# Where the first expert's transposed rows are kept, and in which order the last two attention blocks are routed, in a fused attention, expert and feed-forward kernel

## The chip, the cores and the metric

One NeuronCore of a Trainium2 chip runs the whole kernel. The metric is the device time of one execution in microseconds (us). Five engines work side by side, each through its own queue in order: TensorE (PE, with PEld for its weight loads), VectorE (DVE), ScalarE (ACT), GpSimd (POOL) and SyncE (SP, which only issues transfers here). A matmul shows in the trace as PE; transfers are issued by SP and, where the rows are picked by an index, by POOL.

## The reference, cut to what matters

Attention with four sink keys and a window of 128, then a top-1 mixture of eight experts with a capacity, then a feed-forward layer with a squared relu:

```python
keep = is_sink | in_window                        # q, k, v: 2 x 8 heads x 768 x 64
a = softmax(where(keep, q @ k.T / 8, -1e9)); attn = a @ v
x = attn.transpose(0, 2, 1, 3).reshape(1536, 512)
logits = x @ w_gate; e = argmax(logits, 1); gate = softmax(logits)[e]
disp[e, rank of the token within e] = x[token]    # up to 384 rows of each expert
y = relu(disp @ w1[e]) @ w2[e]                    # 512 -> 1024 -> 512
out_moe[token] = gate * y[e, rank]
h = relu(out_moe @ w_in); out = (h * h) @ w_out   # 512 -> 2048 -> 512
```

The weights w_in and w_out arrive as 64-bit floats and are brought to 32 bits on the chip.

## The kernel before

Every large product is made of three: an operand a is kept as a high part ah (a rounded to the type fp32r) and a low part al = a - ah, and a*b is taken as ah*bh + ah*bl + al*bh. So each operand costs a cast (mostly ACT) and a subtraction (mostly DVE).

**Attention** goes over 12 blocks of 128 tokens, in 48 units of two heads; a unit issues the scores of its own heads and the transposes and value products of earlier ones. For each block, `row` transposes the attended rows to token order (`x`, 128 x 513; the last column will hold the softmax sum), computes the logits `lt`, and queues short DVE steps: `lg` (sum over heads), `mn` (least, since it is negated), `ex` on ACT, the transfer `xd<-x` on SP, `sel`, `fx` (the chosen expert) and `oh` (its one-hot row, L609). `route` (L625) makes the token's rank within its expert: two small matmuls `pos`, a DVE reduction, and in `places` (L638) two DVE compares of the rank with a ramp: `at` for the tables, and for the last two blocks `s0` (for expert 0 only). `invert` (L654) turns `at` into the table `inv` (six matmuls and a DVE addition). The units' follow-up calls stand in `todo`, a table from unit to calls; the calls left for the end come in the order of block and kind.

**The first rows of expert 0** are not gathered as a whole: of blocks 0 to 9 they are gathered from `xd` by an indirect transfer into `xring[0, 0]` (`xb`, L675), and the rows of the blocks 10 and 11 are chosen by a matmul with `s0` (`early`, L691). All three are summed in PSUM in `xT` and, for the softmax sums, in `gate` (L686, L689). Then the memory of the attention (`att`) is released (L829), the pools of the experts are opened, and `pre_split` (L869) casts the sum to the pair `xTs[0]`, tile names xT0h and xT0l, in the pool `moe` that has just been opened. The first matmuls of expert 0 (`h`, L899) need the pair.

**Experts** run one after the other, each in blocks of 128 tokens with `body` (L880); later blocks run only if the count asks for them. While an expert runs, ACT and DVE split the next expert's weights, and the next rows are gathered by POOL (L855) and transposed by PE (`pre`, L865). A result leaves through `ys` and an indirect transfer `yd<-ys` (L957).

**Feed-forward** goes over 3 chunks of 512 tokens and 16 slices f of the hidden layer. `stage_a` (L1099) makes 12 matmuls `a`; ACT takes the relu (L1112), DVE squares it (L1113); `stage_g` (L1124) makes the pair gh (ACT, L1128) and gl (DVE, L1130) in `ghl[f % 2]`; `stage_b` (L1150) makes 12 matmuls `out`. PE's order is a(0), a(1), b(0), a(2), b(1) and so on. In the first chunk each slice also makes one `tick` (L191): a piece of w_in or w_out is shifted and joined by two ACT and four DVE instructions of 1024 columns (L180 to L188). The pool `ffp` of ghl is opened at L1084, just after the pool `moe` is released (L1081).

Of the kernel before, what the change touches and what calls it, by code (L numbers as in the profile page):

```python
# [8 lines left out]
F32 = mybir.dt.float32  # L9
# [7 lines left out]
P = 128  # L17
# [15 lines left out]
def kernel(  # L33
# [591 lines left out]
    def route(n):  # L625
# [12 lines left out]
        def places():  # L638
            if n >= EARLY:
                s0 = ap_.tile([P, P], F32, tag="s0", name="s0", bufs=2)  # L640
                nc.vector.tensor_scalar(s0, place[:, :P], pos, d["oh0"], op0=ALU.is_equal, op1=ALU.mult)
                d["s0"] = s0
            nc.vector.tensor_scalar(at, place, pos, None, op0=ALU.is_equal)
            d["at"] = at

        def take():
            nc.vector.tensor_tensor_reduce(
                out=pj, in0=p_[:, :E], in1=d["oh"], scale=1.0, scalar=0.0, op0=ALU.mult, op1=ALU.add, accum_out=pos
            )
            short.insert(0, places)  # L650

        late.append(take)

    def invert(n):  # L654
        if nblk == 0:
            return
        need(n, "at")
        at, wh = blk[n]["at"], blk[n]["wh"]
# [21 lines left out]
    first = {}  # L680

    def early_sum(a, b, begin, end):

# [5 lines left out]
        nc.tensor.matmul(gp[:, 0:1], b, a[:, DM:], start=begin, stop=end, skip_group_check=True)  # L689

    def early(n):  # L691
        need(n, "s0")
        if n == EARLY:
            first["x"], first["g"] = ps("bg", "xT"), ps("pt", "gate")
        early_sum(blk[n]["x"], blk[n]["s0"], n == EARLY, n == NQB - 1)
        if n == NQB - 2:
            early_sum(xring[0, 0], ident, False, False)

# [142 lines left out]

    xT = {}
    xTs = [tuple(mp.tile([P, KD, P], F32R, name=f"xT{i}{x}") for x in "hl") for i in range(2)]
    gate = [mp.tile([P, 1], F32, name=f"gate{i}") for i in range(4)]

    def x_at(e, b):
        return xring[min(b, XB - 1), e % 2]

    def gate_at(e, b):
        return gate[2 + b % 2 if b else e % 2]  # L850

# [8 lines left out]
    def pre(e, b):  # L860
# [6 lines left out]
        pre_gate(e, b, x_at(e, b)[:, DM:])  # L867

    def pre_split(e, b, p_):  # L869
        xT[e, b] = xTs[min(b, 1)]  # L870
        h_, l_ = (x.rearrange("p c n -> p (c n)") for x in xT[e, b])
        nc.scalar.copy(h_, p_)
        nc.vector.tensor_sub(l_, p_, h_.bitcast(F32))

    def pre_gate(e, b, sums):
        g_ = gate_at(e, b)
        nc.vector.tensor_scalar(g_, sums, 1e-9, None, op0=ALU.add)
        nc.vector.reciprocal(g_, g_)

# [219 lines left out]
    def stage_a(c, f):  # L1099
# [171 lines left out]
```

## Time and profile before

| | us |
|---|---|
| median of 3 runs | 607.14 (607.09 to 607.84) |
| the profiled execution | 608.54 |
| its span, first to last instruction | 606.8 |
| PE busy in it | 575.8 (95%) |
| DVE, ACT, POOL busy | 354.9, 297.2, 136.5 |
| mean granted TensorE clock | 0.989 |

The profile is one execution. Its page gives busy time by engine, groups of instructions, and a chain of waits that ended last; the trace behind it can be asked for a stretch of time by engine (the timeline), for who waited for whom, and for the granted clock in a stretch. In the timeline, a bracket at a row's end is the idle time of the engine just before the row and what ended it. Attention ends at about 133 us, the experts run from 135 to 327 us, the feed-forward layer from 327 us on.

### The profile page before, as it was taken

How to read it: one execution, taken by the hardware profiler on the slowest of the kernel's cores; microseconds unless marked ns; L12 is line 12 of the kernel's file. 1: busy time of each engine (PE TensorE's matmuls, PEld its weight loads, DVE VectorE, ACT ScalarE, POOL GpSimd, SP SyncE). 2: the span in 40 equal slices, each digit the busy share in tenths (PEclk: the TensorE clock that was granted, in tenths of full speed). 3: DMA queues.
4: the chain of work that ended last, by engine and by line, in shares of the span. 5: the costliest groups of instructions: out<-in, count | busy, mean ns of one | idle time of the engine just before them, and what ended most of it. 6: DMA issues, size and time to landing. Idle time of an engine off the chain costs nothing. (4 is left out here: it accounts for less than half of the span.)

```text
span 606.8 us, 9356 instructions
## 1 busy us (share of the span) xinstructions
PE 575.8 (95%) x3243; PEld 458.7 (76%) x3243; DVE 354.9 (58%) x838; ACT 297.2 (49%) x649; POOL 136.5 (22%) x235
## 2 busy tenths in 40 slices
PE   8999999979999999999899899999999999999994
PEld 4777778758887787777687677777888888888883
DVE  3788888747449966957752798996322322322222
ACT  4788878636248756746532455544222221322221
POOL 8544455233223413422211000000200000200002
PEclk9999999989999999999999899999999999999998
DMA  8698996446527985856731946441100000100001
GB/s 186 166 217 162 213 202 150 139 120 196 173 49 241 346 308 151 298 181 215 241 104 57 357 166 199 157 139 52 59 11 1 17 1 0 59 15 2 0 1 60
DMA packets 74625, 82.09 MB, mean 135 GB/s; under 512 B 42200, under 2 KB 53464, under 8 KB 74560
## 3 DMA queue, kind: packets, MB, share of 16 engines
q1 hardware_dynamic: 70608, 72.45, 41.6%
q0 software_dynamic: 3952, 8.82, 4.2%
q8 instruction: 35, 0.57, 0.4%
q14 instruction: 30, 0.25, 0.1%
HBM read 69.29 MB, written 16.08 MB: 141 GB/s over the span
## 5 line engine op out<-in xcount | busy, mean ns | idle before, releaser
L1113 DVE TENSOR_TENSOR xb<-xb 128x512 f32<-128x512 f32 (+1 forms) x48 | 31.6, 658 | 104.6 <-ACT xb L1112 104.6
L1112 ACT ACTIVATE xb<-a 128x512 f32<-128x512 f32 (+1 forms) x48 | 27.6, 575 | 113.8 <-PE a L1110 113.7
L1169 PE MATMUL out<-yl,gh 128*128 128x512 f32 (+1 forms) x188 | 75.8, 403 | 4.1 <-DVE yl L188 4.1
L1169 PE MATMUL out<-yh,gh 128*128 128x512 f32 (+1 forms) x188 | 75.7, 402 | 1.9 <-ACT gh L1128 1.9
L1169 PE MATMUL out<-yh,gl 128*128 128x512 f32 x173 | 68.8, 398 | 0.0
L1128 ACT CAST gh<-xb 128x512 fp32r<-128x512 f32 (+1 forms) x47 | 28.0, 597 | 64.1 <-DVE xb L1113 60.6
L454 ACT ACTIVATE p<-p,nm 128x260 f32<-128x260 f32 (+2 forms) x96 | 46.9, 489 | 17.3 <-DVE nm L442 16.2
L957 POOL DMA_INDIRECT yd<-ys,dst x14 | 26.0, 1857 | 118.7 <-DVE xl L145 33.3
L1130 DVE TENSOR_TENSOR gl<-xb,gh 128x512 fp32r<-128x512 f32 (+1 forms) x47 | 30.7, 653 | 33.8 <-ACT gh L1128 32.5
L1136 POOL DMA_INDIRECT out_dram<-raw,tok x12 | 11.8, 984 | 169.2 <-issue 69.5
L1110 PE MATMUL a<-x2Al,xh 128*128 128x512 f32 (+1 forms) x128 | 47.9, 374 | 0.6 <-DVEq L1078 0.6
L1110 PE MATMUL a<-x2Ah,xh 128*128 128x512 f32 (+1 forms) x128 | 48.2, 376 | 0.3 <-PEq L1078 0.3
L1110 PE MATMUL a<-x2Ah,xl 128*128 128x512 f32 (+1 forms) x128 | 47.8, 374 | 0.0
L1169 PEld LDWEIGHTS out<-yl,gh 128*128 128x128 f32 (+1 forms) x188 | 34.9, 186 | 14.5 <-DVE yl L188 6.2
L145 DVE TENSOR_TENSOR yl<-raw,yh 128x512 fp32r<-128x512 f32 x64 | 40.4, 686 | 5.8 <-ACT yh L144 5.7
L1169 PEld LDWEIGHTS out<-yh,gh 128*128 128x128 f32 (+1 forms) x188 | 34.8, 185 | 10.9 <-ACT gh L1128 2.4
L1169 PEld LDWEIGHTS out<-yh,gl 128*128 128x128 f32 x173 | 32.9, 190 | 8.1 <-DVE gl L1130 0.4
L144 ACT CAST xh<-raw 128x512 fp32r<-128x512 f32 x64 | 36.2, 619 | 1.1 <-DMA raw<-in_moe_w_dram 0.8
L144 ACT CAST yh<-raw 128x512 fp32r<-128x512 f32 x64 | 35.5, 623 | 2.2 <-PEq L969 1.7
L914 DVE TENSOR_TENSOR hTl<-hT,hTh 128x512 fp32r<-128x512 f32 x28 | 19.3, 690 | 28.4 <-ACT hTh L913 28.4
L145 DVE TENSOR_TENSOR xl<-raw,xh 128x512 fp32r<-128x512 f32 x48 | 30.2, 687 | 1.9 <-ACT xh L144 1.6
L529 PE MATMUL ot<-pts,v 128*64 128x128 f32 x352 | 30.1, 286 | 0.5 <-ACT pts L496 0.5
(224 smaller groups left out, 1407.8 us busy)
## 6 DMA issues: line engine op xcount, KB each, us to landing
raw<-in_moe_w_dram SPq DMA_DIRECT2D x64, 512.0 KB, 4.6
raw<-in_moe_w_in_dram SPq DMA_DIRECT2D x16, 512.0 KB, 4.8
raw<-in_moe_w_out_dram SPq DMA_DIRECT2D x8, 1024.0 KB, 5.3
yd<-zero SPq DMA_DIRECT2D x12, 256.5 KB, 6.3
xd<-x SPq DMA_DIRECT2D x12, 256.5 KB, 5.0
xb<-yd SPq DMA_DIRECT2D x12, 256.5 KB, 4.4
kr<-in_k_dram SPq DMA_DIRECT2D x12, 256.0 KB, 5.7
qr<-in_q_dram SPq DMA_DIRECT2D x12, 256.0 KB, 6.2
```

Of the source, the lines that this page charges most:

```text
L144: (hi or nc.scalar.copy)(self.h[i][:, sl], t[:, sl])
L145: (eng or nc.vector).tensor_sub(self.l[i][:, sl], t[:, sl], self.h[i].bitcast(F32)[:, sl])
L454: nc.scalar.activation(d["p"][:, h, :width], d["p"][:, h, :width], AF.Exp, bias=d["nm"][:, h : h + 1], scale=-1.0, accum_out=d["sm"][:, h ...
L529: nc.tensor.matmul(d["o"][i * D : (i + 1) * D, c * P : (c + 1) * P], vt[b, kb][:, h, :], t_, start=i not in d["started"], stop=False, skip ...
L914: nc.vector.tensor_sub(l_, p_, h_.bitcast(F32))
L957: nc.gpsimd.indirect_dma_start(out=yd[:, :], out_offset=bass.IndirectOffsetOnAxis(ap=dst[:, b, e : e + 1], axis=0), in_=y_, in_offset=None ...
L1110: nc.tensor.matmul(a_[:, :w], a, bb[:, kk, :w], start=(kk == 0 and m == 0), stop=(kk == KD - 1 and m == 2))
L1112: nc.scalar.activation(r_, a_[:, :w], AF.Relu)
L1113: nc.vector.tensor_mul(r_, r_, r_)
L1128: nc.scalar.copy(gh[:, :w], r_)
L1130: nc.vector.tensor_sub(gl[:, : w - k_], r_[:, : w - k_], gh.bitcast(F32)[:, : w - k_])
L1169: nc.tensor.matmul(o, a, bb[:, r], start=(f == 0 and m == 0), stop=(f == NFF - 1 and m == len(prods) - 1))
```

## The change

It has three parts.

1. `xTs[0]` and the `gate` tiles are made in the pool `xr`, which lives through the whole kernel, and no longer in the pool of the experts. In the feed-forward layer `ghl[0]` is `xTs[0]` under another view, and only `ghl[1]` is made in `ffp`.
2. `places` is cut in two: `choice` makes `s0`, and `places` makes only `at`. For the blocks 10 and 11 the calls after the last unit are written out in a list: both `row` halves of block 11, `early(10)`, four matmuls on zeros (`wait_with(4)`), `route(11)`, the gathered rows' product, `early(11)`, then `rest` (both `at`, then `pre_split` and `pre_gate` of expert 0), and last both `invert`.
3. `stage_a` issues per kk the products (wh, xh), (wl, xh), (wh, xl) and no longer (wh, xh), (wh, xl), (wl, xh). In the very first slice all eight with xh come first, then the four with xl.

```diff
         def places():
-            if n >= EARLY:
-                s0 = ap_.tile([P, P], F32, tag="s0", name="s0", bufs=2)
-                nc.vector.tensor_scalar(s0, place[:, :P], pos, d["oh0"], op0=ALU.is_equal, op1=ALU.mult)
-                d["s0"] = s0
             nc.vector.tensor_scalar(at, place, pos, None, op0=ALU.is_equal)
             d["at"] = at
+
+        def choice():
+
+            s0 = ap_.tile([P, P], F32, tag="s0", name="s0", bufs=2)
+            nc.vector.tensor_scalar(s0, place[:, :P], pos, d["oh0"], op0=ALU.is_equal, op1=ALU.mult)
+            d["s0"], d["places"] = s0, places
...
-            short.insert(0, places)
+            short.insert(0, choice if n >= EARLY else places)
...
+    xTs = [tuple(xrp.tile([P, KD, P], F32R, name=f"xT0{x}") for x in "hl")]
+
+    gate = [xrp.tile([P, 1], F32, name=f"gate{i}") for i in range(4)]
...
     def early(n):
         need(n, "s0")
         if n == EARLY:
             first["x"], first["g"] = ps("bg", "xT"), ps("pt", "gate")
         early_sum(blk[n]["x"], blk[n]["s0"], n == EARLY, n == NQB - 1)
-        if n == NQB - 2:
-            early_sum(xring[0, 0], ident, False, False)
+
+    def rest():
+
+        for n in range(EARLY, NQB):
+            blk[n].pop("places")()
+            need(n, "at")
+        pre_split(0, 0, first["x"])
+        pre_gate(0, 0, first["g"][:, 0:1])
...
-        for n in range(EARLY, NQB):
-            todo[max(todo)].append((n, 2.5, lambda n=n: early(n)))
+
+
+        a, z = EARLY, NQB - 1
+        todo[max(todo)] = [
+            (0, 0, lambda: need(a, "s0")), (1, 0, lambda: row(z, 0)), (2, 0, lambda: row(z, 1)), (3, 0, lambda: early(a)),
+            (4, 0, lambda: wait_with(4)), (5, 0, lambda: route(z)), (6, 0, lambda: early_sum(xring[0, 0], ident, False, False)),
+            (7, 0, lambda: early(z)), (8, 0, rest), (9, 0, lambda: invert(a)), (10, 0, lambda: invert(z)),
+        ]
...
+    def wait_with(k):
+        p_ = ps("ot", "fill")
+        for _ in range(k):
+            nc.tensor.matmul(p_, zb[:, :P], zb, start=True, stop=True)
...
-    xTs = [tuple(mp.tile([P, KD, P], F32R, name=f"xT{i}{x}") for x in "hl") for i in range(2)]
-    gate = [mp.tile([P, 1], F32, name=f"gate{i}") for i in range(4)]
+    xTs.append(tuple(mp.tile([P, KD, P], F32R, name=f"xT1{x}") for x in "hl"))
...
     W[1].alloc()
-    if nblk:
-        pre_split(0, 0, first["x"])
-        pre_gate(0, 0, first["g"][:, 0:1])
     load_x(0, 1)
...
-    ghl = [tuple(ffp.tile([P, CH], F32R, name=f"g{x}{i}") for x in "hl") for i in range(2)]
+    ghl = [tuple(x.rearrange("p c n -> p (c n)") for x in xTs[0]), tuple(ffp.tile([P, CH], F32R, name=f"g{x}1") for x in "hl")]
...
+        prods = []
         for kk in range(KD):
             r = slice(f % 2 * 512 + kk * P, f % 2 * 512 + kk * P + P)
             wh, wl = WI.h[f // 2][:, r], WI.l[f // 2][:, r]
-            for m, (a, bb) in enumerate(((wh, xh), (wh, xl), (wl, xh))):
-                nc.tensor.matmul(a_[:, :w], a, bb[:, kk, :w], start=(kk == 0 and m == 0), stop=(kk == KD - 1 and m == 2))
+            prods += [(wh, xh[:, kk, :w]), (wl, xh[:, kk, :w]), (wh, xl[:, kk, :w])]
+        if (c, f) == (0, 0):
+
+            prods = [x for i, x in enumerate(prods) if i % 3 < 2] + prods[2::3]
+        for i, (a, bb) in enumerate(prods):
+            nc.tensor.matmul(a_[:, :w], a, bb, start=i == 0, stop=i == len(prods) - 1)
```

How the instructions stand on the engines is shown at three places. First DVE at the end of attention, from the rank of block 10 (`pos`) to the one-hot row of block 11 (`oh`); `s` is s0, `sel` and `fx` lead to the choice. Before:

```order
L647 ISA pj,pos<-pos,oh 128x8
L647 ISA pos 128x1
L583 TENSOR_TENSOR lt<-xr,r 128x32 x2
L641 TENSOR_SCALAR s_2393<-place,pos,oh_2351 128x128
L643 TENSOR_SCALAR at<-place,pos 128x384
L663 TENSOR_TENSOR inv<-inv 128x24
L617 TENSOR_REDUCE lg<-lt 128x8
L604 TENSOR_REDUCE mn<-lg 128x1
L619 SCALAR_TENSOR_TENSOR sel<-lg,mn,rev 128x8
L620 TENSOR_REDUCE fx<-sel 128x1
L609 TENSOR_SCALAR oh<-rev,fx 128x8
```

And the same place in the changed kernel:

```order
L649 ISA pj,pos<-pos,oh 128x8
L649 ISA pos 128x1
L645 TENSOR_SCALAR s_2378<-place,pos,oh_2357 128x128
L583 TENSOR_TENSOR lt<-xr,r 128x32 x2
L617 TENSOR_REDUCE lg<-lt 128x8
L604 TENSOR_REDUCE mn<-lg 128x1
L619 SCALAR_TENSOR_TENSOR sel<-lg,mn,rev 128x8
L620 TENSOR_REDUCE fx<-sel 128x1
L609 TENSOR_SCALAR oh<-rev,fx 128x8
```

`s` has gone ahead of `lt`; `at` and the addition to `inv`, which needs PE's `inv` matmuls, have left the place between `lt` and `lg` and now stand behind block 11's `s`.

Second PE in the same stretch, from the product that chooses block 10's rows (`xT<-s,x`, L686 before, L694 after). Before:

```order
L686 MATMUL xT<-s_2393,x 128x128 x4
L689 MATMUL gate<-x,s_2393 128x1
L686 MATMUL xT<-ident,xb_197 128x128 x4
L689 MATMUL gate<-xb_197,ident 128x1
L662 LDWEIGHTS at
L662 MATMUL inv<-wh,at 128x8
...
L631 MATMUL pos<-oh,tri 128x8
...
L686 MATMUL xT<-s_2434,x 128x128 x4
L689 MATMUL gate<-x,s_2434 128x1
```

And in the changed kernel:

```order
L694 MATMUL xT<-s_2378,x 128x128 x4
L697 MATMUL gate<-x,s_2378 128x1
L789 LDWEIGHTS zb
L789 MATMUL fill<-zb 128x512
...
L631 MATMUL pos<-oh,tri 128x8
...
L694 MATMUL xT<-ident,xb_203 128x128 x4
L697 MATMUL gate<-xb_203,ident 128x1
L694 MATMUL xT<-s_2436,x 128x128 x4
L697 MATMUL gate<-x,s_2436 128x1
L666 LDWEIGHTS at
L666 MATMUL inv<-wh,at 128x8
```

The gathered rows' product has moved behind `pos` of block 11, the `inv` matmuls of both blocks behind all of `xT`, and four matmuls on zeros stand ahead of `pos`.

Third ACT at the start of the feed-forward layer, with what each instruction waits for: the first two relus and the first two high parts. Before:

```order
L186 CAST yh_5318<-raw_75 128x1024 [waits DVE_49,PE_49]
L1112 ACTIVATE xb_199<-a 128x512 [waits DMASW4_49,PE_49]
L1128 CAST gh_5338<-xb_199 128x512 [waits DMASW3_49,DMASW4_49,DMASW2_49,DMASW5_49,DMASW1_49,DMASW6_49,DMASW0_49,DMASW7_49,DVE_49,Pool_49]
L180 ACTIVATE raw_76<-raw_76 128x1024 [waits DMAHW5_49,DMAHW4_49]
L1112 ACTIVATE xb_203<-a 128x512 [waits DMASW0_49,PE_49]
L1128 CAST gh_5340<-xb_203 128x512 [waits DVE_49]
```

And in the changed kernel:

```order
L186 CAST yh_5323<-raw_75 128x1024 [waits DVE_49,PE_49]
L1139 ACTIVATE xb_205<-a 128x512 [waits DMASW4_49,PE_49]
L1155 CAST xT0h<-xb_205 128x512 [waits DVE_49]
L180 ACTIVATE raw_76<-raw_76 128x1024 [waits DMAHW5_49,DMAHW4_49,Activation_49]
L1139 ACTIVATE xb_209<-a 128x512 [waits DMASW0_49,PE_49]
L1155 CAST gh_5343<-xb_209 128x512 [waits DMASW4_49,DMASW3_49,DMASW5_49,DMASW2_49,DMASW6_49,DMASW1_49,DMASW7_49,DVE_49,Pool_49]
```

The waits for POOL's transfers (DMASW) have moved from the first high part to the second.

## Rows read from the trace of the kernel before

**Rows 1.** The page, busy time: engine, us, share of the span, instructions.
```profile
PE 575.8 (95%) x3243; PEld 458.7 (76%) x3243; DVE 354.9 (58%) x838; ACT 297.2 (49%) x649; POOL 136.5 (22%) x235
```

**Rows 2.** Waits of PE, whole span: us in total, times, longest.
```profile
PE out L1169 <- DVE yl L188: 4.1, 6, 0.9
```

**Rows 3.** Timeline of PE, end of attention and first expert: start, us, instruction.
```profile
127.20 1.16 PE L686 MATMUL xT<-s,x 128*128 128x128 f32 x8 [0.54 <-DVE s L641]
128.33 1.14 PE L686 MATMUL xT<-ident,xb 128*128 128x128 f32 x8
...
131.18 0.17 PE L631 MATMUL pos<-oh,tri 128*128 128x8 bf16 x1 [1.44 <-DVE oh L609]
...
132.12 1.57 PE L686 MATMUL xT<-s,x 128*128 128x128 f32 x8 [0.75 <-DVE s L641]
...
135.37 0.80 PE L899 MATMUL h<-xh,xT0h 128*128 128x512 f32 x1 [0.40 <-DMA raw<-in_moe_w_dram]
...
139.38 0.45 PE L899 MATMUL h<-xh,xT0h 128*128 128x512 f32 x1
...
146.58 1.04 PE L865 MATMUL xT<-ident,xb 128*128 128x128 f32 x8
```

**Rows 4.** Timeline of DVE, end of attention.
```profile
126.70 0.19 DVE L583 TENSOR_TENSOR lt<-xr,r 128x32 f32<-128x32 f32 x1 [0.30 <-PE xr L572]
...
129.78 0.18 DVE L663 TENSOR_TENSOR inv<-inv 128x24 f32<-128x24 f32 x1 [1.94 <-PE inv L662]
129.88 0.26 DVE L617 TENSOR_REDUCE lg<-lt 128x8 f32<-128x64 f32 x1
```

**Rows 5.** Timeline of ACT (first row) and POOL, end of attention.
```profile
134.73 0.59 ACT L872 CAST xT0h<-xT 128x512 fp32r<-128x512 f32 x1 [3.98 <-DMA xd<-x]
...
127.02 1.30 POOL L589 TENSOR_TENSOR x<-x,r 128x256 f32<-128x256 f32 x2 [1.42 <-ACT x L588]
...
135.13 1.04 POOL L855 DMA_INDIRECT xb<-xd,src  x1 [3.47 <-DVE cntf L828]
```

**Rows 6.** Line L855 (gathers of rows) from 118 to 160 us.
```profile
DMA to landing us min/median/max: 2.9/4.2/4.8
```

**Rows 7.** Stretches: length, busy us (count) by engine, clock, DMA share, GB/s.
```profile
130.00:132.00 2.00, 0.19 (x2) 0.10 (x1) 1.57 (x10) 0.39 (x2) 0.42 (x2) 1.00 0.18 63
...
134.00:136.00 2.00, 1.60 (x8) 0.56 (x5) 1.16 (x6) 1.27 (x3) 0.87 (x1) 0.50 0.84 268
```

**Rows 8.** Timeline of PE, early attention: matmuls on zeros.
```profile
9.37 1.04 PE L754 MATMUL fill<-zb 128*128 128x512 bf16 x4
```

**Rows 9.** Timeline of DVE and of POOL at 122 us.
```profile
122.78 0.38 DVE L619 SCALAR_TENSOR_TENSOR sel<-lg,mn,rev 128x8 f32<-128x8 f32 x1
...
122.53 0.61 POOL L589 TENSOR_TENSOR x<-x,r 128x256 f32<-128x256 f32 x1 [1.05 <-ACT x L588]
```

**Rows 10.** Timeline of PE, start of the feed-forward layer.
```profile
327.67 0.47 PE L1110 MATMUL a<-x2Ah,xh 128*128 128x512 f32 x1 [0.30 <-PEq L1078]
328.76 0.50 PE L1110 MATMUL a<-x2Al,xh 128*128 128x512 f32 x1 [0.63 <-DVEq L1078]
...
336.35 0.50 PE L1169 MATMUL out<-yh,gh 128*128 128x512 f32 x1 [1.94 <-ACT gh L1128]
...
341.06 0.40 PE L1110 MATMUL a<-x2Ah,xh 128*128 128x512 f32 x1
```

**Rows 11.** Timeline of DVE (first row) and ACT, same place.
```profile
332.27 0.69 DVE L1113 TENSOR_TENSOR xb<-xb 128x512 f32<-128x512 f32 x1 [2.24 <-ACT xb L1112]
...
335.68 0.62 ACT L1128 CAST gh<-xb 128x512 fp32r<-128x512 f32 x1 [3.44 <-DMA yd<-ys,dst]
```

**Rows 12.** The chain that ended last, in order of time: start, us, what.
```profile
356.08 1.23 DVE raw L183
...
362.20 1.23 DVE raw L183
...
418.69 2.80 PE out L1169 x12
```

More of the change, by code (lines that the diff above doesn't have):

```diff
@@ L656, in invert @@
             return
+        if "places" in blk[n]:
+            blk[n].pop("places")()
         need(n, "at")
@@ L689, in early_sum, with gate_at, pre_split, pre_gate @@
         nc.tensor.matmul(gp[:, 0:1], b, a[:, DM:], start=begin, stop=end, skip_group_check=True)
+    xT = {}
+    def gate_at(e, b):
+        return gate[2 + b % 2 if b else e % 2]
+    def pre_split(e, b, p_):
+        xT[e, b] = xTs[min(b, 1)]
+        h_, l_ = (x.rearrange("p c n -> p (c n)") for x in xT[e, b])
+        nc.scalar.copy(h_, p_)
+        nc.vector.tensor_sub(l_, p_, h_.bitcast(F32))
+    def pre_gate(e, b, sums):
+        g_ = gate_at(e, b)
+        nc.vector.tensor_scalar(g_, sums, 1e-9, None, op0=ALU.add)
+        nc.vector.reciprocal(g_, g_)
     def early(n):
@@ L695, in early @@
         early_sum(blk[n]["x"], blk[n]["s0"], n == EARLY, n == NQB - 1)
-        if n == NQB - 2:
-            early_sum(xring[0, 0], ident, False, False)
+    def rest():
+        for n in range(EARLY, NQB):
+            blk[n].pop("places")()
+            need(n, "at")
+        pre_split(0, 0, first["x"])
+        pre_gate(0, 0, first["g"][:, 0:1])
     XB = 3
@@ L840 @@
     W[1].pool, W[E], WO.pool = wy, WI, wy
-    xT = {}
-    xTs = [tuple(mp.tile([P, KD, P], F32R, name=f"xT{i}{x}") for x in "hl") for i in range(2)]
-    gate = [mp.tile([P, 1], F32, name=f"gate{i}") for i in range(4)]
+    xTs.append(tuple(mp.tile([P, KD, P], F32R, name=f"xT1{x}") for x in "hl"))
     def x_at(e, b):
         return xring[min(b, XB - 1), e % 2]
-    def gate_at(e, b):
-        return gate[2 + b % 2 if b else e % 2]
     def load_x(e, b):
@@ L867, in pre @@
         pre_gate(e, b, x_at(e, b)[:, DM:])
[L869 to L878, printed above, removed]
     def body(e, b, splits, plan, also):
```

## The prediction

> **What bounds the kernel now.** The page's busy times come first: PE is at work for 575.8 of 606.8 us, 95% [rows 1], so what can be won must come from the few places where PE stands idle or runs at the lower clock, and from anything that sets PE's pace without leaving a long gap. The list of PE's waits names such a pace-setter: six waits for the low parts of the weights made on DVE (yl, L188), 4.1 us in all [rows 2]. The timelines of the two transitions show the rest.
>
> At the end of attention PE goes through short products with gaps. It waits 0.54 us for s0 of block 10, 1.44 us for block 11's one-hot row, 0.75 us for block 11's s0 [rows 3]. The one-hot row is late because DVE, in order, stands 1.94 us in front of the addition to `inv`, whose matmuls lie on PE behind all of block 10's and the gathered rows' products; only then comes lg of block 11, although its input lt was ready long before [rows 4]. Then the cast of xT0h waits on ACT until 134.73 us, and the row says for what: the transfer `xd<-x`, which reads memory of the attention that the tile is laid over [rows 5]. In 130 to 132 us PE is busy for 0.19 of 2.00 us at granted clock 1.00; in 134 to 136 us the clock is 0.50, the level of 1.2 GHz [rows 7]. The first nine products of expert 0 take from 135.37 to 139.38 us, 4.01 us [rows 3], where twelve later on take 2.80 us [rows 12].
>
> At the start of the feed-forward layer PE waits 0.63 us for DVE after the first product, and 1.94 us for gh of slice 0 [rows 10]. On ACT that cast waits for the transfer `yd<-ys`: its input, DVE's square, is ready at 332.27 + 0.69 = 332.96 us, it begins at 335.68 us [rows 11].
>
> **The change, part by part.** *DVE's order at the end of attention.* With `at` and `inv` gone from between, lg can follow lt at 126.70 + 0.19 = 126.9 us, not 129.88 us [rows 4]. From lg to the matmul pos it took 131.18 - 129.88 = 1.30 us [rows 3, 4], so pos could go at 128.2 us.
>
> *PE's order there.* s0 of block 10 now precedes lt and falls into a stretch in which DVE waited for PE, so the 0.54 us wait goes and the choice of block 10 starts at 127.20 - 0.54 = 126.66 us. Its five instructions take 128.33 - 127.20 = 1.13 us [rows 3], to 127.8. The four matmuls on zeros are an addition: four took 1.04 us with the drain of the last [rows 8], I take 0.95, to 128.75. They, not DVE, now decide when pos goes: 0.55 us are given away here, for a PE that is not idle. From pos to the choice of block 11 it took 132.12 - 131.18 = 0.94 us [rows 3], which gives 129.7; the gathered rows' product, moved into this gap, ends at 128.8 + 1.13 = 129.95 and decides. With 1.13 us for the choice of block 11, the sum is ready at 131.1 us.
>
> *The cast.* With xT0h outside the released memory the cast starts then and takes 0.59 us [rows 5]. On PE the twelve `inv` matmuls, `cnt` and two matmuls on zeros cover that time; they are short beside it. The first product of expert 0 goes at 131.85 us against 135.37: 3.5 us. The wait for the released memory does not vanish: it passes to ACT's first weight cast of expert 1, with the relu of expert 0 queued behind. Its end was at 134.73; the transfer leaves after ex, the row's softmax sum, which moves ahead by up to 3.0 us with lg, and after POOL's products for x, which end at 127.02 + 1.30 = 128.32 us [rows 5], so by my estimate it lands before 133 us, and the relu is not due before 134.7. Nothing on the path.
>
> *The clock.* PE has no gap of more than some tenths left between 126.66 and 131.85 us. If the clock stays at 1.00, nine products cost 9 x 2.80 / 12 = 2.1 us and 0.1 for the first one, not 4.01: 1.8 us more. Where the clock falls anyway the gain of this term is nothing. I take 1.8, since the one stretch before the fall that differs from the others is the one with 0.19 us of work [rows 7]. DVE's xT0l and the first weight splits stand closer now; 0.1 off. **First transition: 3.5 + 1.8 - 0.1 = 5.2 us.**
>
> *A lock.* At 122.78 us the instruction sel took 0.38 us and ended at 123.16, just when POOL's product for x, begun at 122.53, ended (123.14) [rows 9]. In the changed kernel sel and oh of block 11 run at about 127.3 to 128.2 us, beside POOL's two products from 127.02 to 128.32 [rows 5]; before, they ran after them. The bound is nothing, and 128.32 - 127.3 = 1.0 us if DVE waits for both. The cover is the 0.55 us of the matmuls on zeros, so it costs 0 to 0.5 us, and I take 0, as the row at 122 us shows a wait for one product only. The Trainium skill (SBUF — State Buffer, section Who interferes with whom) says that GpSimd and a DVE instruction with two SBUF inputs, or in a two-port mode, exclude each other for the whole instruction; by it sel and oh would each wait, and the sum would be 8.2 us in place of 8.7. The row at 122 us agrees for sel.
>
> *Tables later.* src, for the gathers by POOL, now follows xT0l on DVE: at about 133.1 us. The gathers began at 135.13 [rows 5] and can begin at 133.7; with 1.04 us to issue and 4.8 us at most to land [rows 6] the first is there at 139.6. PE uses it at 146.58 - 5.2 = 141.4 us [rows 3]. Covered by 1.8 us, no cost.
>
> *stage_a.* Eight products that need only the high part come first, so PE does not wait for DVE after the first one: 0.63 us and the restart, 0.8 us together (328.76 against 328.0, [rows 10]). The order of the other slices has the same products at the same price: nothing.
>
> *gh of slice 0.* Relu and square follow 0.8 us earlier, and the cast comes right behind the square: 335.68 - 332.96 = 2.7 us [rows 11], with the above 3.5 us. The wait for `yd<-ys` passes to gh of slice 1, whose input comes some 5 us after that of slice 0, near 337 us, since a slice with its tick takes DVE up to 6.1 us [rows 12]; the transfer has landed by 335.68 [rows 11]: hidden. For PE alone this would be worth more: 1.94 + 0.8, and 12 products between 336.35 and 341.06 us took 4.71 us [rows 10], not 2.80, another 1.9: 4.6 us. But in the ticks DVE sets the pace: one slice takes it 362.20 - 356.08 = 6.1 us, PE's 24 products take 5.6 [rows 12], and PE waits for yl [rows 2]. DVE's chain starts with gl of slice 0 and moves by 3.5 us; PE will meet it at the first yl, and wait there the longer. **Second transition: 3.5 us**, between 2.5 (if the longer idle lowers the clock and PE is late for DVE's next squares) and 4.6.
>
> *xTs[0] for its whole life and the change of addresses* add no instruction: nothing.
>
> **The sum** is 5.2 + 3.5 = 8.7 us. Between the two, PE waits for hardly anything but its own results, so the first gain should pass through the experts. Against the profiled execution, 608.54 us (span 606.8 and 1.7 around it), this makes 599.8. That execution lies 1.4 us above the median of the runs, 607.14; from the median the forecast is **598.4 us**.
>
> **The rivals.** (1) *The clock falls all the same* at the beginning of expert 0. For it: the products at the end of attention are short, and the cast still leaves PE little but small matmuls. Against it: the clock was still 1.00 on the mean of 130 to 132 us, after 0.19 us of work [rows 7]. 607.14 - 6.9 = 600.2 us. (2) *A released-memory wait returns with another tile* of the same pools (ACT's first weight cast, gh of slice 1), so that one transition gains little: 607.14 - 5.2 = 601.9 at the second, 603.6 at the first. The waits shown by the order speak for its being possible, the two margins above against it. (3) *The lock at its full price*: 598.9, inside the forecast's own range. (4) *PE keeps all of its 4.6 us* in the second transition: 597.3; DVE's 6.1 us speak against it. (5) *Slower*: the rows for the second block of expert 0 come late, because their index table now stands behind xT0l and `at` on DVE. Up to a landing at 141.4 us this costs nothing; beyond it PE waits, and only from 141.4 + 8.7 = 150.1 us is the kernel slower than before. The gathers would have to land 16 us after their issue, where 4.8 is the most seen. At a landing at 152 us it is 609 us.
>
> **How the numbers follow.** Forecast with (3): 0.66, own range 597.6 to 599.3. (1): 0.14. (2): 0.08. (4): 0.06. Slower, by (5) or a like delay of the weights: 0.03; no change to be told, 0.03. The low end takes in (4) with some tenths for the runs' own spread, 597.0; the high end takes in (1) and the low bound of the second transition, 601.4. A measurement of this kernel can tell 0.2%, 1.2 us, from no change: faster 0.94, same 0.03, slower 0.03.
>
> **What would show it.** In the timeline of the changed kernel: lg of block 11 near 126.9 us; PE without a gap of 1 us from 126 to 132; xT0h's cast right behind the last xT product; the first h at 131.5 to 132.3 and a granted clock of 1.00 in the following 4 us; then a shift that stays near 5 us through the experts. At the feed-forward start: no wait after the first product; gh's cast (now named xT0h) right behind the square; b(0) right behind a(1); the first wait for yl longer than before, some 1 to 2 us; and DVE's L183 rows 3.5 us closer to the start of the layer. A clock of 0.50 at the first h, or a wait of PE for a gather at 141 us, would make it wrong; so would a first weight cast on ACT that waits past 135 us.

## The result and the profile after

| | before | after |
|---|---|---|
| median of the comparison, us | 607.49 (607.09 to 609.78, 4 runs) | 599.79 (599.34 to 601.79, 4 runs) |
| ratio, 95% interval | | 0.9873 [0.9847, 0.9899] |
| the profiled execution, us | 608.54 | 599.34 |
| its span, mean granted clock | 606.8, 0.989 | 597.6, 0.998 |

The change makes the kernel 7.7 us faster. The forecast was 598.4 us, with a range from 597.0 to 601.4. The rows of after follow in the order in which the argument rested on those of before.

The page's busy times, to set beside [rows 1]: PE has 4.2 us less, at a higher clock, and 9.2 us less span.

```profile
PE 571.6 (96%) x3245; PEld 456.2 (76%) x3247; DVE 354.2 (59%) x838; ACT 296.7 (50%) x649; POOL 138.8 (23%) x235
```

Timeline of PE at the end of attention, to set beside [rows 3]:

```profile
126.49 1.05 PE L694 MATMUL xT<-s,x 128*128 128x128 f32 x8
...
127.52 1.02 PE L789 MATMUL fill<-zb 128*128 128x512 bf16 x3
128.38 0.17 PE L631 MATMUL pos<-oh,tri 128*128 128x8 bf16 x1
...
129.55 1.14 PE L694 MATMUL xT<-s,x 128*128 128x128 f32 x8
...
131.36 0.50 PE L924 MATMUL h<-xh,xT0h 128*128 128x512 f32 x1
```

No row carries a bracket: the three waits of 0.54, 1.44 and 0.75 us are gone, and the first product of expert 0 comes at 131.36 instead of 135.37 us. Why, is on DVE, ACT and POOL (timelines of these three engines, to set beside [rows 4] and [rows 5]):

```profile
126.92 0.27 DVE L617 TENSOR_REDUCE lg<-lt 128x8 f32<-128x64 f32 x1
...
127.41 0.23 DVE L619 SCALAR_TENSOR_TENSOR sel<-lg,mn,rev 128x8 f32<-128x8 f32 x1
...
130.72 0.59 ACT L707 CAST xT0h<-xT 128x512 fp32r<-128x512 f32 x1 [2.92 <-PE xT L694]
133.11 1.66 ACT L144 CAST yh<-raw 128x512 fp32r<-128x512 f32 x3 [1.80 <-DVE off L1063]
134.72 0.60 ACT L927 ACTIVATE hs<-h 128x512 f32<-128x512 f32 x1
...
127.00 1.18 POOL L589 TENSOR_TENSOR x<-x,r 128x256 f32<-128x256 f32 x2 [1.43 <-ACT x L588]
...
133.37 1.04 POOL L891 DMA_INDIRECT xb<-xd,src  x1 [4.47 <-DVE off L1065]
```

lg follows lt at once. The cast waits for PE's sum. Behind it ACT's first weight cast now stands idle for 1.80 us, until 133.11 us. The prediction had let the wait for released memory pass to this cast; the profile names DVE's `off` here, which the cast does not read, so that it is the same wait is likely, not shown. The relu of expert 0 follows these casts at 134.72 us, and PE's transposes of its result go at 135.92 us without a wait in front of them. Two stretches, to set beside [rows 7] (length, busy us and count by engine, granted clock, DMA share, GB/s):

```profile
130.00:132.00 2.00, 2.00 (x26) 1.39 (x24) 0.66 (x2) 0.59 (x1) 0.00 (x0) 1.00 0.79 168
134.00:136.00 2.00, 2.00 (x10) 1.54 (x10) 1.61 (x10) 1.83 (x4) 1.41 (x2) 1.00 0.46 136
```

PE is at work without a pause and the clock stays at its upper level, 2.4 GHz, where it stood at 1.2 before. At the start of the feed-forward layer (timelines of PE, ACT and DVE, to set beside [rows 10] and [rows 11]):

```profile
322.20 0.47 PE L1137 MATMUL a<-x2Ah,xh 128*128 128x512 f32 x1 [0.30 <-PEq L1100]
322.51 0.39 PE L1137 MATMUL a<-x2Ah,xl 128*128 128x512 f32 x1
...
327.86 0.40 PE L1196 MATMUL out<-yh,xT0h 128*128 128x512 f32 x1
...
339.66 0.51 PE L1196 MATMUL out<-yh,xT0h 128*128 128x512 f32 x1 [0.43 <-ACT yh L186]
341.10 0.50 PE L1196 MATMUL out<-yl,xT0h 128*128 128x512 f32 x1 [0.93 <-DVE yl L188]
...
326.62 0.62 ACT L1155 CAST xT0h<-xb 128x512 fp32r<-128x512 f32 x1 [0.76 <-DVE xb L1140]
...
325.90 0.69 DVE L1140 TENSOR_TENSOR xb<-xb 128x512 f32<-128x512 f32 x1 [1.33 <-ACT xb L1139]
...
328.68 1.23 DVE L183 SCALAR_TENSOR_TENSOR raw<-raw 128x1024 int32<-128x1024 int32 x1
...
345.65 0.70 DVE L181 TENSOR_SCALAR raw<-raw 128x1024 int32<-128x1024 int32 x1 [0.22 <-DMA raw<-in_moe_w_out_dram]
```

The waits of 0.63 and 1.94 us are gone, and gh of slice 0 (now xT0h) follows the square. PE meets the pace of the weight pieces at 339.66 us (waiting for ACT's yh) and 341.10 us (for DVE's yl). The last row is new: DVE waits for a piece of w_out. The profile's chain that ended last runs through this wait, and before it through SP's twelve transfers of zeros to the output. Waits of PE in the first chunk, to set beside [rows 2]:

```profile
PE out L1196 <- DVE yl L188: 4.9, 6, 0.9
```

### The profile page after: what moved, and what is told of

It is laid out like the page before. It is cut to its first block, busy times and chain, and to the rows that moved or that the text cites. A ratio compares the mean times of both kernels' runs of the same rounds, so it can differ in the third digit from the quotient of the medians.

```text
span 597.6 us, 9362 instructions
## 1 busy us (share of the span) xinstructions
PE 571.6 (96%) x3245; PEld 456.2 (76%) x3247; DVE 354.2 (59%) x838; ACT 296.7 (50%) x649; POOL 138.8 (23%) x235
## 5 line engine op out<-in xcount | busy, mean ns | idle before, releaser
L1196 PE MATMUL out<-yl,xT0h 128*128 128x512 f32 (+1 forms) x96 | 38.6, 402 | 4.9 <-DVE yl L188 4.9
L1196 PE MATMUL out<-yh,xT0h 128*128 128x512 f32 (+1 forms) x96 | 38.8, 405 | 0.4 <-ACT yh L186 0.4
L1196 PE MATMUL out<-yh,gh 128*128 128x512 f32 (+1 forms) x92 | 36.4, 395 | 0.0
L1196 PE MATMUL out<-yl,gh 128*128 128x512 f32 (+1 forms) x92 | 36.3, 395 | 0.0
L1196 PE MATMUL out<-yh,xT0l 128*128 128x512 f32 x88 | 34.8, 396 | 0.0
L1196 PE MATMUL out<-yh,gl 128*128 128x512 f32 x85 | 33.7, 396 | 0.0
L1155 ACT CAST xT0h<-xb 128x512 fp32r<-128x512 f32 (+1 forms) x24 | 14.3, 596 | 30.7 <-DVE xb L1140 30.7
L1155 ACT CAST gh<-xb 128x512 fp32r<-128x512 f32 (+1 forms) x23 | 13.7, 596 | 31.9 <-DVE xb L1140 31.9
```

Source lines behind the costliest of these rows:

```text
L1155: nc.scalar.copy(gh[:, :w], r_)
L1196: nc.tensor.matmul(o, a, bb[:, r], start=(f == 0 and m == 0), stop=(f == NFF - 1 and m == len(prods) - 1))
```

## The experiments

One table serves all of them: starts read from PE's timeline of each profile, in us. "h" is the first product of expert 0, "e1" that of expert 1, "a" that of the feed-forward layer, "yl" the last wait of PE for a low half of weights; "tail" is span minus yl.

| kernel | h | e1 | a | yl | span | tail |
|---|---|---|---|---|---|---|
| before | 135.37 | 174.84 | 327.67 | 413.03 | 606.8 | 193.8 |
| before_again | 135.79 | 174.42 | 327.26 | 412.79 | 606.5 | 193.7 |
| b_zeros | 135.58 | 173.70 | 326.52 | 412.24 | 607.7 | 195.5 |
| b_zeros_again | 134.76 | 172.64 | 326.57 | 411.82 | 606.8 | 195.0 |
| b_pair_kept | 133.90 | 172.83 | 325.58 | 411.32 | 604.6 | 193.3 |
| b_order_only | 133.02 | 170.87 | 323.67 | 409.12 | 602.8 | 193.7 |
| after | 131.36 | 169.45 | 322.20 | 404.34 | 597.6 | 193.3 |
| after_again | 131.30 | 169.44 | 322.19 | 404.86 | 598.1 | 193.2 |
| a_no_fill | 131.18 | 169.33 | 321.98 | 403.85 | 597.1 | 193.3 |
| a_ghl_swapped | 131.31 | 169.52 | 322.33 | 408.02 | 601.3 | 193.3 |
| a_no_highfirst | 131.32 | 169.46 | 322.12 | 404.62 | 597.9 | 193.3 |
| a_xl_pool | 131.32 | 169.44 | 322.45 | 411.06 | 604.4 | 193.3 |
| a_lead | 132.96 | 171.09 | 323.99 | 404.93 | 598.4 | 193.5 |
| a_lead_spread | 131.32 | 169.48 | 322.16 | 401.56 | 594.8 | 193.2 |

The theory is that of the prediction. Its rivals were the clock, the released memory, and PE instead of DVE as the pace of the first chunk.

### Both kernels once more

> The kernel before itself, for a second trace of it. Theory: first product of h at 135.4 us, clock at 0.50 to 0.66 in 132 to 140 us and again at 0.50 to 0.86 in 336 to 342 us, last wait for a low half of weights at 413.0 us, 193.3 to 193.8 us from there to the end, as in the first trace (each within 0.4 us); time 607 to 609 us. Rival: the clock falls in the first transition only in some runs: then one of the two traces has h's first output 1.6 us earlier.

> The changed kernel itself, on the chip of the other runs of this group, so that they can be set against it like for like. Theory: its gain over the kernel before is that of its trace, 8.7 us, ratio 0.9857; rival: the 7.7 us of the first comparison (0.9873) is the better figure, since some gain is lost behind 404 us to something that the change brings.

before_again: 606.99 us (606.20 to 611.40, 12 runs). Its trace has the clock fall in both transitions again, and its starts in the table lie within 0.5 us of the first trace's. Its twelve runs go from 606.20 us at a mean granted clock of 0.995 to 611.40 at 0.984, nearly in step: how much the clock falls differs from run to run. The two profiles, 0.989 and 0.988, are ordinary ones: the median of the 73 runs of before beside the experiments is 0.989.

after_again: 600.20 us (6 runs), ratio 0.9889 [0.9870, 0.9907]. This ratio makes 6.7 us of 607.87, while the two medians lie 7.7 us apart, as in the first comparison. The pairs of traces give 8.7 and 7.9 us at yl. The second is smaller since DVE waits longer for w_out there (0.22 us in after):

```profile
346.14 0.70 DVE L181 TENSOR_SCALAR raw<-raw 128x1024 int32<-128x1024 int32 x1 [0.72 <-DMA raw<-in_moe_w_out_dram]
```

Nothing is lost behind yl: the changed kernel's tails are 0.5 us shorter than those of before (why is open), so the rival's reason falls. What is left is within the scatter of such medians. The twelve runs of before_again have a median 1.3 us below that of 23 other runs of the same kernel in the same comparison (608.27). And the median of all 77 runs of before, 608.27, lies 8.1 to 8.5 us above the two medians of the changed kernel.

### The first transition: where the pair lies, in which order the blocks go, and the clock

> The kernel before with xTs[0] and gate in the lasting pool, nothing moved; in the feed-forward layer slice 0's pair stays in the pool that is opened there and slice 1's is xTs[0]. Theory: the cast of xT0h begins when the last xT product is done, about 133.75 us in place of 134.73, so 1.0 us is won at the first product; the gaps stay, so the clock falls as before; slice 0's cast waits for yd<-ys as before: about 606.4. Rival (the released memory is what the first transition waits for): 3 us or more.

```diff
-    xTs = [tuple(mp.tile([P, KD, P], F32R, name=f"xT{i}{x}") for x in "hl") for i in range(2)]
+    xTs = [tuple(xrp.tile([P, KD, P], F32R, name=f"xT0{x}") for x in "hl")]
...
+    xTs.append(tuple(mp.tile([P, KD, P], F32R, name=f"xT1{x}") for x in "hl"))
```

Measured 607.45 us, ratio 0.9972 [0.9953, 0.9991]. Timeline of ACT, and stretches:

```profile
133.26 0.58 ACT L873 CAST xT0h<-xT 128x512 fp32r<-128x512 f32 x1 [2.53 <-PE xT L688]
...
130.00:132.00 2.00, 0.19 (x2) 0.10 (x1) 1.58 (x10) 0.39 (x2) 0.41 (x2) 1.00 0.20 70
132.00:134.00 2.00, 1.68 (x19) 1.52 (x20) 0.71 (x6) 0.58 (x1) 0.00 (x0) 0.86 0.98 187
134.00:136.00 2.00, 2.00 (x6) 1.57 (x6) 1.76 (x12) 1.54 (x3) 0.84 (x1) 0.50 0.89 323
```

The cast no longer waits for the transfer, and h comes 1.5 us earlier where 1.0 was expected. The ratio makes 1.7 us of 608.65, so the rival, 3 us or more for the memory alone, does not hold. The clock falls as before; PE's empty stretch (0.19 us of work in 2) is still there.

> The changed kernel with the pair xTs[0] and the gates back in the experts' pool, the split of the sum behind the release as before, both pairs of slices in the feed-forward pool, no high-parts-first: of the change only the order of the last two blocks is left. Theory: the sum xT is complete at 130.7 us as in the changed kernel, the cast waits for the landing of xd<-x at about 132, the first product goes at 132.7, 2.7 us before 135.4; with the clock at 1.00 another 1.8: 4.5 us faster than before, about 602.9; if PE's longer gap lowers the clock, 2.7 us. Rival (without the memory the order is worth nothing, since the transfer ends last): under 1 us.

```diff
+            (0, 0, lambda: need(a, "s0")), (1, 0, lambda: row(z, 0)), (2, 0, lambda: row(z, 1)), (3, 0, lambda: early(a)),
+            (4, 0, lambda: wait_with(4)), (5, 0, lambda: route(z)), (6, 0, lambda: early_sum(xring[0, 0], ident, False, False)),
```

The lines are those of the change that stay: the order of the last two blocks with the four matmuls on zeros (and, in `stage_a`, the order of the three products per kk); the pairs are back in the pools of before. Measured 604.73 us, ratio 0.9939 [0.9915, 0.9962], 3.7 us where 4.5 was expected. Timelines of ACT and PE, and a stretch:

```profile
132.38 0.58 ACT L705 CAST xT0h<-xT 128x512 fp32r<-128x512 f32 x1 [4.10 <-DVE cntf L865]
...
133.02 0.50 PE L921 MATMUL h<-xh,xT0h 128*128 128x512 f32 x1 [0.96 <-DMA raw<-in_moe_w_dram]
...
132.00:134.00 2.00, 1.04 (x4) 0.55 (x4) 1.23 (x8) 1.62 (x4) 1.04 (x1) 1.00 0.85 309
```

The clock stays at 1.00, though the cast still comes late (132.38, against 130.72 with the pair kept). The bracket names DVE's cntf, which a cast of xT does not read. That it is the released memory here as well is likely: in b_pair_kept the place of the pair alone turned the cast's wait into one for PE. By e1, against the first trace of before, the order is worth 4.0 us, the pair 2.0, both together 5.4.

> The kernel before, with matmuls on zeros put into PE's gaps at the end of attention (6 ahead of pos of block 11, 3 ahead of block 11's choice, 5 in place of 2 ahead of expert 0); nothing else is moved. Theory (the clock term is a cost of its own, caused by the gaps): the first product of expert 0 still goes at about 135.4 us, but the granted clock stays at 1.00 and the first nine products take 2.2 us, not 4.0: 1.8 us faster than the kernel before where that one's clock falls, about 605.5. Rival (the clock falls there whatever PE does, or its fall costs nothing in the end): no difference, or up to 0.5 us slower for the zeros in the way.

> The kernel before with matmuls on zeros in the gaps, once more, beside the kernel before of the same chip. In the first trace expert 1 started 1.14 us earlier than in the kernel before, and yet the median of the whole was 1.1 us higher. Theory: the clock gain is real and reaches the end; the higher median came from a scatter of 2 to 3 us behind 412 us that has nothing to do with the edit: this time 0.8 to 1.4 us below the kernel before. Rival: the matmuls on zeros bring a cost of their own behind 412 us: again 0.5 to 1.5 us above it.

```diff
-NWARM = 2
+NWARM = 5
...
+    todo[max(todo)] += [(z, 1.9, lambda: wait_with(6)), (z, 2.2, lambda: wait_with(3))]
```

The first expectation missed: 609.75 us beside 608.65 for before, ratio 1.0026 [1.0002, 1.0050]. The second run gave 609.01 beside 608.27, ratio 1.0013 [0.9992, 1.0034]: its interval takes in no difference, its median lies where the rival of the second expectation put it. The clock did stay up: both traces have 1.00 in every stretch from 126 to 140 us, such as this one of the first:

```profile
134.00:136.00 2.00, 1.58 (x10) 0.60 (x6) 0.95 (x5) 1.06 (x3) 0.36 (x1) 1.00 0.89 246
```

And e1 comes 1.1 and 1.8 us, yl 0.8 and 1.0 us earlier than in the kernel before of the same number. But both have one pause that none of the other twelve traces shows, here from PE's timelines of the first and the second:

```profile
526.38 0.35 PE L1117 MATMUL a<-x2Ah,xl 128*128 128x416 f32 x1 [1.57 <-issue]
```

```profile
525.54 0.35 PE L1117 MATMUL a<-x2Ah,xl 128*128 128x416 f32 x1 [1.15 <-issue]
```

It stands at a product with 416 columns, in the branch that the last chunk's width selects, and the tails are 195.5 and 195.0 us, 1.7 and 1.3 us longer than those of before. Why an edit near 130 us goes with a pause there is not known.

> The changed kernel without the four matmuls on zeros that it puts ahead of block 11's position product. Theory: with the new order TensorE has work every 1 to 2 us in this stretch anyway, so the clock stays at 1.00 from 126 to 142 us without them; the position product and the choice come up to 0.4 us earlier, the first h product is at 131.0 to 131.4 us (131.36 with them), and the time is that of the changed kernel within 0.4 us. Rival: the matmuls on zeros are what holds the clock; without them a stretch of 2 us at or below 0.86 appears between 128 and 138 us, the first output of expert 0 (h at 131.36, y at 137.75 in the changed kernel) is 1.5 to 2 us later, and so is the end.

```diff
-            (4, 0, lambda: wait_with(4)), (5, 0, lambda: route(z)),
+            (4, 0, lambda: wait_with(0)), (5, 0, lambda: route(z)),
```

599.50 us (4 runs), ratio 0.9875 [0.9857, 0.9893], h at 131.18. The theory holds: the changed order alone keeps PE at work, and the four matmuls on zeros add nothing. Their stretch without them:

```profile
128.00:130.00 2.00, 1.79 (x17) 1.79 (x17) 1.45 (x7) 0.00 (x0) 0.54 (x3) 1.00 0.44 147
```

### The second transition

> The changed kernel with the two pairs of slices exchanged: slice 0's pair is the one in the feed-forward pool, slice 1's is xTs[0]. Theory: slice 0's cast waits for yd<-ys again, 2.7 us, DVE's chain of ticks starts 2.7 us later, and as DVE sets the pace there the kernel is 2.4 to 2.8 us slower than the changed one, about 602.4; PE's clock falls behind the gap but that is hidden in the wait for yl. Rival (PE sets the pace): 4 us slower, gap and clock, about 603.8; rival (high-parts-first is what counted): under 1 us slower.

```diff
-    ghl = [tuple(x.rearrange("p c n -> p (c n)") for x in xTs[0]), tuple(ffp.tile([P, CH], F32R, name=f"g{x}1") for x in "hl")]
+    ghl = [tuple(ffp.tile([P, CH], F32R, name=f"g{x}0") for x in "hl"), tuple(x.rearrange("p c n -> p (c n)") for x in xTs[0])]
```

603.28 us (6 runs), ratio 0.9909 [0.9886, 0.9933]: 3.1 to 3.5 us above the changed kernel's two medians (1.2 to 2.2 us by the ratios, each to its own runs of before), and 3.2 to 3.7 in the traces at yl. Timelines of ACT and PE, and a stretch:

```profile
330.63 0.62 ACT L1155 CAST gh<-xb 128x512 fp32r<-128x512 f32 x1 [4.63 <-DMA yd<-ys,dst]
...
331.30 0.50 PE L1196 MATMUL out<-yh,gh 128*128 128x512 f32 x1 [3.13 <-ACT gh L1155]
...
334.00:336.00 2.00, 2.00 (x6) 1.59 (x5) 1.77 (x2) 0.20 (x1) 0.00 (x0) 0.50 1.10 385
```

With slice 0's pair back in released memory the wait for `yd<-ys` is back, and with it PE's idle time and the lower clock. The cast begins 4.0 us later than in after (330.63 against 326.62), where 2.7 was foreseen. What is left of it at yl lies between the theory (2.4 to 2.8) and the rival with PE as the pace (4), so this run does not decide between the engines. From "a" to "yl" it takes 85.69 us, no less than the 85.36 of before: all of the second transition's gain hangs on where this one pair lies.

> The changed kernel with the first slice's products of the FFN in the old order (the products on the low part between those on the high part, not behind them). Theory: the first chunk's low part is written at about 324.6 us (1.22 us of VectorE from 323.34), so the third product, which needs it, waits: TensorE's first products stop for about 1 us behind 322.9 us, the square at 325.90 is some 0.8 us later, and as VectorE sets the pace up to 404 us the end is 0.8 us later than in the changed kernel. Rival: VectorE is not the pace there, or the low part is early enough: 0 to 0.2 us.

```diff
-        if (c, f) == (0, 0):
-
-            prods = [x for i, x in enumerate(prods) if i % 3 < 2] + prods[2::3]
```

599.65 us (4 runs), ratio 0.9873 [0.9856, 0.9890]: no different from the changed kernel. Timelines of PE and DVE:

```profile
323.22 0.50 PE L1134 MATMUL a<-x2Al,xh 128*128 128x512 f32 x1 [0.41 <-DVEq L1100]
...
326.48 0.69 DVE L1137 TENSOR_TENSOR xb<-xb 128x512 f32<-128x512 f32 x1 [2.00 <-ACT xb L1136]
```

PE's wait is back and the square is 0.58 us later than the 325.90 of after, but DVE's wait of 0.22 us for w_out at 345.65 is not there, and yl is only 0.3 us behind that of after (0.2 ahead of after_again). The rival's number holds, but neither of its reasons does: what DVE gains by the earlier square it loses to the wait for w_out. Where that wait is missing, as in a_no_fill too, the first slice's order counts: from "a" to "yl" it takes 81.87 us with it (a_no_fill) and 82.50 without (a_no_highfirst).

### Who sets the pace of the first chunk

> The changed kernel with one VectorE operation of the FFN's first half moved to GpSimd: the low half of each w_in piece from the third on (six subtractions of 1.22 us on VectorE from 333.71 us on; GpSimd takes 1.28 us for half the size, so about 2.6 us each). Theory (VectorE sets the pace from 326 to 404 us, TensorE only waits for it): TensorE's waits for yl, 4.9 us in six, go to under 1 us, the last of them comes 4 us or more earlier than at 404.34 us, and the time is 4 to 5 us below the changed kernel's, about 595 us. Rival 1: GpSimd beside VectorE's 1.2-us operations on two operands slows them, VectorE's saving of 7.3 us is eaten, and the gain is under 1 us or a loss. Rival 2: TensorE is the pace there already: no difference (within 0.5 us).

```diff
-            nc.vector.tensor_sub(w.l[f], lo.bitcast(F32), w.h[f].bitcast(F32))
+            (nc.gpsimd if kind == "i" and f >= 2 else nc.vector).tensor_sub(w.l[f], lo.bitcast(F32), w.h[f].bitcast(F32))
```

607.16 us (12 runs), ratio 0.9991 [0.9973, 1.0009]: 7 us lost, rival 1. Timelines of POOL and DVE, and the group of L183 in 322 to 410 us (busy us, mean ns):

```profile
333.84 2.52 POOL L188 TENSOR_TENSOR xl<-raw,xh 128x1024 fp32r<-128x1024 f32 x1 [8.17 <-ACT xh L186]
...
334.83 2.60 DVE L183 SCALAR_TENSOR_TENSOR raw<-raw 128x1024 int32<-128x1024 int32 x1 [0.79 <-ACT raw L180]
...
L183 DVE SCALAR_TENSOR_TENSOR raw<-raw 128x1024 int32<-128x1024 int32 x12 | 22.9, 1907 | 4.9 <-ACT raw L180 4.8
```

L183 takes 1.22 us alone. POOL's subtraction ends at 336.36 us, and the L183 beside it takes 2.60 us and ends 1.07 us after that. Six times 1.38 us more is 8.3 us, which pays back DVE's 7.3 us saved, and the waits for ACT come on top. This is what the Trainium skill says in SBUF — State Buffer, Who interferes with whom: a DVE instruction with two SBUF inputs and a GpSimd instruction that reads SBUF exclude each other. The trace agrees here.

> The changed kernel with one further move in the FFN's first 13 slices: VectorE's shift of the next weight piece (0.69 us) stands between the square and the low half of the square, where VectorE now sits idle 0.69 us for ScalarE's cast, instead of behind the low half. No work is added or taken away. Theory (VectorE sets the pace there): a slice takes it 5.46 us instead of 6.15, less than TensorE's 24 products (24 times 0.236 is 5.66 us), so TensorE sets the pace, its waits for weight parts (5.3 us in seven) go to under 1 us, and the end comes 4 to 5.3 us earlier, at 594.5 to 596 us. Rival 1: the pieces' transfers are late then (VectorE already waited 0.22 us for one): the shift waits for them and the low half behind it, gain 1 to 3 us. Rival 2: TensorE is the pace already: within 0.5 us.

```diff
         nc.scalar.copy(gh[:, :w], r_)
+        if c == 0 and f < NFF - 2:
+            lead()
...
```

`lead` issues the shift of the next piece (L181 in after), which is then left out of its old place. 599.09 us (6 runs), ratio 0.9842 [0.9809, 0.9875]. From "a" to "yl" it takes 80.94 us, not the 82.14 of after or the 82.67 of after_again: 1.2 to 1.7 us, and rival 1 is in the trace (DVE):

```profile
344.45 0.69 DVE L1150 TENSOR_TENSOR xb<-xb 128x512 f32<-128x512 f32 x1
347.19 0.70 DVE L180 TENSOR_SCALAR raw<-raw 128x1024 int32<-128x1024 int32 x1 [2.05 <-DMA raw<-in_moe_w_out_dram]
```

> The kernel with the shift ahead of the low half, and with the twelve transfers that fill the output with zeros issued one per slice from the third slice on, instead of all twelve ahead of the FFN (SyncE spent 11.02 us on them from 325.8 us, and the DMA engines' busy share was 0.94 to 1.09 in 332 to 346 us). Theory (the weight pieces queue behind these transfers): VectorE's wait of 2.05 us for a piece at 345 us goes, expert 1's start to the last wait for a low half is set by TensorE, and from the FFN's first product to the last wait for a low half it takes 78 to 79 us instead of 80.94 (82.14 in the changed kernel); the time is 1.5 to 2.5 us below that of the kernel with the early shift alone, 596.5 to 597.5 us. Rival: the transfers, spread over the slices, delay the later pieces as much: 0 to 0.5 us.

```diff
             tick()
+            if f >= 2 and fills:
+                fills.pop(0)()
...
```

This is a_lead with one thing more: `fills` holds the twelve transfers of zeros to the output, which the changed kernel issues one behind the other from 325.56 us on (timeline of SP). 596.54 us (596.45 to 596.60, 5 runs) beside 608.44 for before, ratio 0.9802 [0.9776, 0.9829], the fastest of all: the wait of 2.05 us is gone, "a" to "yl" takes 79.40 us. The time is as expected, this stretch is not quite (78 to 79), and PE still waits for DVE in it (0.57 us at yl). It is not 76.8, which the 5.3 us of PE's waits promised, since a slice takes DVE 348.56 - 342.63 = 5.93 us, not 5.46. It now waits 0.33 us for ACT's cast of the weight piece (DVE):

```profile
342.63 0.68 DVE L1152 TENSOR_TENSOR xb<-xb 128x512 f32<-128x512 f32 x1
343.23 0.69 DVE L180 TENSOR_SCALAR raw<-raw 128x1024 int32<-128x1024 int32 x1
344.00 0.69 DVE L1171 TENSOR_TENSOR gl<-xb,gh 128x512 fp32r<-128x512 f32 x1
345.02 1.22 DVE L198 TENSOR_TENSOR xl<-raw,xh 128x1024 fp32r<-128x1024 f32 x1 [0.33 <-ACT xh L196]
...
348.56 0.68 DVE L1152 TENSOR_TENSOR xb<-xb 128x512 f32<-128x512 f32 x1
```

So DVE did set the pace: in after a slice takes it 6.12 us, so 13 slices are 2.5 us shorter here, the 0.22 us for w_out are gone, and "a" to "yl" is 2.7 us shorter. Spreading the zeros without the early shift was not run; my estimate is that it could give no more than the 0.22 to 0.72 us that DVE waits in after and after_again.

## Why the prediction came out as it did

**First transition, 5.2 us: in the trace 5.4 us** (e1, 5.0 between the second traces). lg came at 126.92 (126.9 forecast), pos at 128.38 (128.75), the first gather at 133.37 (133.7), h at 131.36 (131.85, though the steps as written, 131.1 + 0.59, make 131.7). The steps hold. The 0.37 us at pos are small parts: the choice of block 10 began 0.17 us earlier, took 1.03 us for 1.13, and the matmuls on zeros 0.86 for 0.95. Each part alone gives less than both, 2.0 and 4.0 us.

**The clock, 1.8 us.** That it stays up was right, and an order without an empty stretch is enough for it (a_no_fill, b_order_only). From h to the first product of y it took 143.35 - 135.37 = 7.98 us before and 6.39 after, so 1.6 us in the first pair of traces; in before_again 0.7 of it is left behind h, as the clock fell earlier there. b_zeros, which keeps the clock up and moves nothing, has 1.1 and 1.8 us at e1, but no shorter time in the end.

**The lock, taken at 0.** sel took 0.23 and oh 0.27 us beside POOL's two products from 127.00 to 128.18; sel took 0.23 with POOL idle too (before, 130.37). So neither waited here, and nothing of the price of up to 0.5 us was paid. A wait was possible all the same: in a_lead's trace (timelines of DVE and POOL) sel took 0.58 us beside a single product and ended with it.

```profile
128.32 0.58 DVE L629 SCALAR_TENSOR_TENSOR sel<-lg,mn,rev 128x8 f32<-128x8 f32 x1
...
128.27 0.61 POOL L599 TENSOR_TENSOR x<-x,r 128x256 f32<-128x256 f32 x1 [0.22 <-ACT x L598]
```

What decides between 0.23 and 0.58 is not settled. The cover was smaller than forecast: oh is ready at 128.21 us and pos goes at 128.38, so 0.2 us and not 0.55; another 0.3 us lies in front of block 11's choice, where s0 is ready at 129.21 and the product begins at 129.55. A wait of 0.35 us would still have been hidden, one of 1.0 us not.

**Tables and gathers.** Covered, as forecast: PE's waits have none for a gather of the experts' rows (`xb<-xd`).

**stage_a, 0.8 us, and gh of slice 0, 2.7 us.** Both are in the trace where they arise. From "a" to the square it took 4.60 us before (327.67 to 332.27) and 3.70 after: 0.9 us, of which a_no_highfirst (4.36) gives 0.66 to the first slice's order. From "a" to DVE's first L183 it took 10.06 us before (timeline of DVE) and 6.48 after, 3.6 us where 3.5 was forecast.

```profile
337.73 1.23 DVE L183 SCALAR_TENSOR_TENSOR raw<-raw 128x1024 int32<-128x1024 int32 x1
```

But the shift grows from 5.47 us at "a" to only 8.69 at yl, so 3.2 us, and from 5.07 to 7.93, 2.9 us, in the second pair. The step that failed here is that DVE's chain would carry all of it to the end. The prediction put the transfers of w_out at nothing, and the earlier DVE waits for one of them: 0.22 us in after, 0.72 in after_again, not in a_no_fill, and in no trace of before. So it differs from execution to execution. a_ghl_swapped gives 3.2 to 3.7 us at yl for the pair alone. PE meets DVE with waits of 0.43 and 0.93 us, 1.4 in all where 1 to 2 was said, and not PE's 4.6 us but DVE's move decided.

**The sum** of 8.7 us is what the traces show, 8.69 and 7.93 us at yl, and 9.2 and 8.4 over the whole span. That the first meets it to the hundredth is luck: the first transition gave 0.2 us more than forecast, the second 0.3 us less, and 0.5 us behind yl was not foreseen. From the profile the forecast was 599.8, and 599.34 to 600.20 came out. **The step that failed most is the last one**, which took off 1.4 us because the profile of before lay above the median of three runs. Over 77 runs of before, in five comparisons, the medians were 607.49 to 608.65, and 608.27 over all; 607.14 was a low one, as is the 606.99 of before_again's twelve, and the profile, 608.54, lay near the middle. There is a second reason, which is argued and not shown: the clock's falls, which the change takes away, are a part of what makes runs of before differ, so that at 0.995 there was less to win than in the profile at 0.989. (The mean clock is a rough gauge, since it counts falls behind PE's last product too: in after 0.50 from 596 us on.) A gain that consists in part of such falls can't be taken in full from the median of runs that do not all have them.

## What to carry to other kernels

Look first in memory that is reused across a stage's end: one pair of tiles there cost 2 us at one place and over 3 at another, and the wait shows up under the name of a transfer which the instruction doesn't use. When work is put earlier in a queue, see whether a transfer or another engine is close behind, as that is where the gain stops. On the engine that sets the pace, filling its idle 0.7 us per slice by order alone, with the transfers in its way spread out, gained 2.7 us, while handing 7.3 us of its work to GpSimd lost 7.

## What the runs showed of the hardware

**The clock can fall after equal work.** a_lead differs from after only in the feed-forward layer. Stretches of after, and then of a_lead:

```profile
124.00:126.00 2.00, 1.59 (x19) 1.32 (x14) 0.72 (x6) 0.37 (x1) 1.53 (x3) 1.00 0.48 152
```

```profile
124.00:126.00 2.00, 1.59 (x15) 1.32 (x12) 0.72 (x5) 0.37 (x1) 1.47 (x3) 0.86 0.55 149
126.00:128.00 2.00, 2.00 (x11) 2.00 (x11) 0.77 (x4) 0.55 (x2) 0.56 (x1) 0.50 0.34 109
```

PE was busy for 1.59 us in both, and in one the clock fell, as in none of the other twelve traces at that place; h came 1.6 us later there (132.96). The five other runs of a_lead are 0.9 to 2.1 us faster than this one (600.11), so this is likely one source of the scatter among runs of one kernel.

**A pause far from the edit.** The pause of 1.15 to 1.57 us near 526 us is in both traces of a kernel whose edits end at 136 us, and in no other trace. What ties it to them is not known.
